# Low halves of w_in (from its seventh piece) and of the first layer's outputs: made by VectorE instead of GpSimd

## The chip, the cores and the metric

The kernel runs on one core of one Trainium2 chip. The metric is the device time of one execution in microseconds (us). The engines are TensorE (PE in the profile; PEld is its weight load), VectorE (DVE), ScalarE (ACT), GpSimd (POOL) and SyncE (SP), which here only issues DMAs. Each engine works through its own instructions strictly in the order of the program; only semaphores tie them together. "The time" below is the median of three runs; the profile is one further execution.

## What is computed

Three layers, chained:

```python
# attention with a decaying state, per batch and head (4 x 8, 768 steps, 48 wide)
f = sigmoid(f_logit)
state = f[t] * state + outer(k[t], v[t]);  y[t] = q[t] @ state
# x: the 3072 tokens, 384 wide
h = x @ w_in                      # 384 -> 2048
g = maximum(0.01 * h, h)
x2 = g @ w_out                    # 2048 -> 384
# then 8 experts, each with the 384 tokens that a greedy assignment gives it
out[mask] = maximum(x2[mask] @ w1[e], 0) @ w2[e]
```

The result has to be about as exact as float32. So the large products are made from pairs of 16-bit numbers: a value is split into a high half (the value rounded to float16) and a low half (what the rounding left out, again as float16), and a product is three matmuls, high by high, high by low and low by high. The low halves are the subject of this change.

## The kernel before

Tokens come in 24 tiles of 128. Three tiles make a group of 384, so there are eight groups. For each tile the attention runs as a chain over PE, ACT and DVE; its matmuls write to the tiles P (decays), A (scores), kT (turned keys), U (state update) and y, and DVE makes `ks`, `qs`, `de`, `St`, `am`, `ahl`, `vl` and `ys` for it. Its result is turned by a DMA into `xT`.

The first layer (`first`) goes over the 16 slices of 128 columns of w_in. Each slice f of a group is nine matmuls into one of three PSUM buffers `hp`; ACT scales it into `g`, DVE finishes the maximum there (which frees the buffer), and after every second f ACT makes the high half `gh` of both slices and POOL or DVE the low half `gl` of both. The second layer (`second`) takes, for each tile of tokens and each f, three matmuls into `xp` from `gh`, `gl` and the two halves of w_out, `wo`. Order on PE: layer one of group 0, layer one of group 1, layer two of group 0, layer one of group 2, and so on; attention of later tiles is put between.

The weights arrive as 64-bit words and are rebuilt to float32 by three integer instructions on DVE for each piece (`as_f32`: one TENSOR_SCALAR, two SCALAR_TENSOR_TENSOR, all 128 x 384; tiles `winu` and `woutu`). There are 16 pieces of w_in and 16 of w_out. For a piece of w_in (`split_win`) ACT then writes the high half `winh`, ACT writes the scaled float32 value once more into `wsc`, and POOL subtracts: `winl = wsc - winh`. For a piece of w_out (`split_wout`) ACT writes the high half and DVE the low half straight from the rebuilt words. The pieces pass through three load buffers (tag `ws`); a load into one waits until the piece three before has been rebuilt.

What sets the order: the opening (the string START) is written out by hand and kept in program order; it ends about where the first group's matmuls are under way. After it, a small driver hands out the work by due times, and a scheduler places each instruction by priorities and its own estimate of when operands are ready. So a changed instruction can move its neighbours.

Of the kernel before, what the change touches and what calls it, by code (L numbers as in the profile page):

```python
# [15 lines left out]
OP = mybir.AluOpType  # L16
# [5 lines left out]
SX, SWI, SG, SWO = 2.0 ** 10, 2.0 ** 7, 2.0 ** 10, 2.0 ** 8  # L22
# [69 lines left out]
def body(tc, qk, v, f_logit, w_in, w_out, w_gate, w1, w2, out):  # L92
    nc = tc.nc
    w_in, w_out = w_in.bitcast(I32), w_out.bitcast(I32)
    PE, DVE, ACT, POOL, SP = (InOrder(tc, e) for e in (nc.tensor, nc.vector, nc.scalar, nc.gpsimd, nc.sync))
# [10 lines left out]
    GW = 384  # L106
    RT = 3
    NWD = 0
    NWARM, WU = 0, 4
    MP = (1,)  # L110
    LEAD, PACE0, W0, POOLN, GLN, FT, KP, PB = 3, 1300.0, 1000.0, 8, 2, 8, 4, 3

    with ExitStack() as ctx:
        consts = ctx.enter_context(tc.tile_pool(name="consts", bufs=1))
# [15 lines left out]
        def mm(o, l, r, start, stop):  # L130
            return PE.matmul(o, l, r, start=start, stop=stop, skip_group_check=True)

        def copy(o, i, scale=1.0):
            return ACT.activation(o, i, AF.Copy, bias=0.0, scale=scale)
# [115 lines left out]
        winh = wpool.tile([128, KT, FF], F16)  # L250
        winl = wpool.tile([128, KT, FF], F16)
# [3 lines left out]
        def as_f32(t, name):  # L255

            sh = [128, t.shape[1], t.shape[2]]
            u = aw.tile(sh, I32, name=name + "u", tag="wu", bufs=WU)
            DVE.tensor_scalar(u, t[:, :, :, 1], 3, 0x3FFFFFFF, op0=OP.logical_shift_left, op1=OP.bitwise_and)
            DVE.scalar_tensor_tensor(u, t[:, :, :, 0], 29, u, op0=OP.logical_shift_right, op1=OP.bitwise_or)  # L260
            DVE.scalar_tensor_tensor(u, t[:, :, :, 1], -0x40000000, u, op0=OP.bitwise_and, op1=OP.bitwise_or)
            return u.bitcast(F32)

        def split_win(i):
            s = slice(i * WIC, (i + 1) * WIC)
            r = as_f32(w_in_s.pop(i), "win")
            yield
            t = aw.tile([128, KT, WIC], F32, name="wsc", tag="wsc", bufs=WU)
            copy(winh[:, :, s], r, SWI)
            copy(t, r, SWI)  # L270
            yield
            POOL.tensor_tensor(winl[:, :, s], t, winh[:, :, s], op=OP.subtract)
# [266 lines left out]
        def first(gi, nn, gx):  # L539
            xh, xl = gx[:, :KT], gx[:, KT:]  # L540
            N = 128 * nn
            gp = g2pool[0] if gi == LAST else gpool
            gh = gp.tile([128, NF, GW], F16, name="gh")
            gl = gp.tile([128, NF, GW], F16, name="gl")
            gh_[gi], gl_[gi] = gh, gl
            for f in range(NF):
                while ("in", f * NPC // NF) not in ready:
                    yield None
                fs = slice(128 * f, 128 * (f + 1))
                hp = psum.tile([128, GW], F32, name="hp", tag="mm", bufs=3)[:, :N]  # L550
                for c in range(KT):
                    mm(hp, winh[:, c, fs], xh[:, c, :N], c == 0, False)
                    yield N / 2.4
                    mm(hp, winh[:, c, fs], xl[:, c, :N], False, False)
                    yield N / 2.4
                    mm(hp, winl[:, c, fs], xh[:, c, :N], False, c == KT - 1)
                    if c < KT - 1:
                        yield N / 2.4
                a = SG / (SX * SWI)
                with tc.high_priority():  # L560
                    if f % 2 == 0:
                        g = work.tile([128, 2, GW], F32, name="g32")
                    t = g[:, f % 2, :N]
                    i = copy(t, hp, 0.01 * a)
                    fed.append((i, DVE.scalar_tensor_tensor(t, hp, a, t, op0=OP.mult, op1=OP.max)))
                    big[0] += 3 * KT
                    if f % 2:
                        s = slice(f - 1, f + 1)
                        copy(gh[:, s, :N], g[:, :, :N])
                        (POOL if gi == 0 or (gi < GLN and f % 4 == 1) else DVE).tensor_tensor(  # L570
                            gl[:, s, :N], g[:, :, :N], gh[:, s, :N], op=OP.subtract)
                yield N / 2.4

        def tok(n):
# [508 lines left out]

        live, complete = {}, set()
        names = dict(f=s0, v=s0v, p=s1, k=s2, a=s3, y=s4, x=s5, w=split_win)

        def group_x(n):
# [113 lines left out]
        def layer1():  # L1201
            for g in range(len(groups)):
                while not all(n in attended for n in groups[g]):
                    yield None
                started.append(g)
                if g == LAST:
                    while "experts" not in ready or "gate" not in ready:
                        yield None
                    ctxL.close()
                    g2pool.append(pool(ctxL, "g2", "left"))  # L1210
                    ctxP.close()
                    banks[0] = ctxP.enter_context(tc.tile_pool(name="banks2", bufs=1, space=bass.MemoryType.PSUM,
                                                               reuse_waits="tile"))
                beside = chain(*(logits(k) for k in LATE[:-1])) if g == LAST else iter(())
                for x in first(g, len(groups[g]), GX[g]):
                    yield x
                    if x is not None:
                        yield next(beside, 0.0)
                yield from beside
                done[0] = g + 1  # L1220
                if g > 0 and g - 1 not in LATE:
                    for m, n in enumerate(groups[g - 1]):
                        yield from second(g - 1, n, m)
            yield from logits(LAST)
# [105 lines left out]
```

## Time and profile before

| what | value |
| --- | --- |
| time, median of 3 runs | 785.66 us (784.7 to 787.34) |
| profiled execution, its own time | 781.42 us |
| its span, first to last instruction | 779.6 us |
| PE busy | 730.7 us (94%) |
| DVE busy | 558.8 us (72%) |
| ACT busy | 350.0 us (45%) |
| POOL busy | 142.7 us (18%), 158 instructions |

The profiled execution lies 4.2 us below the median of the runs, and 1.8 us of its time lie outside the span. The 72% of DVE is a mean over stages of very different kinds: from 47 to about 150 us DVE is busy nearly without a break, later it has room. POOL works in the opening and in this stage, and then not again before 400 us.

### The profile page before, as it was taken

What the parts mean: (1) busy time and instruction counts of PE and PEld (TensorE: products, weight loads), DVE (VectorE), ACT (ScalarE), POOL (GpSimd) and SP (SyncE); (2) the same over time, 40 slices, a digit from 0 to 9 for tenths busy, and PEclk for the clock granted to TensorE, in tenths of its full rate; (3) what the DMA queues carried; (4) which work ended last, traced back from release to release, by engine and by line L of the source; (5) the groups of instructions that cost most, each with busy time, mean ns of one, the idle gap of its engine ahead of it and who ended that gap; (6) DMA issues with size and microseconds to landing.
All of it is one profiled execution on the core that took longest, in us unless ns stands there. A gap on an engine that the chain in (4) does not pass through costs nothing.

```text
span 779.6 us, 15455 instructions
## 1 busy us (share of the span) xinstructions
PE 730.7 (94%) x5900; PEld 484.1 (62%) x5900; DVE 558.8 (72%) x1579; ACT 350.0 (45%) x732; POOL 142.7 (18%) x158
## 2 busy tenths in 40 slices
PE   6888998999999999998999999999989899999995
PEld 5756775677576577676666666555545455556663
DVE  5899999968966967966873958677685676873320
ACT  6566656557755754753663743000123123222320
POOL 5355312000000000000000001010243434535111
PEclk9899899999999999999999999999999999999998
DMA  9965544698897798998898500050475557665300
GB/s 258 249 162 164 161 133 125 152 276 219 237 249 213 210 309 191 250 249 221 238 272 230 166 2 2 23 192 22 148 224 155 177 158 168 228 198 174 107 31 30
DMA packets 111643, 135.90 MB, mean 174 GB/s; under 512 B 62929, under 2 KB 94674, under 8 KB 109522
## 3 DMA queue, kind: packets, MB, share of 16 engines
q1 hardware_dynamic: 106194, 100.31, 49.1%
q0 software_dynamic: 5376, 34.61, 13.1%
q8 instruction: 46, 0.75, 0.4%
q14 instruction: 27, 0.22, 0.1%
HBM read 86.52 MB, written 34.60 MB: 155 GB/s over the span
## 4 chain that ended last, share of the span: by engine, by line
PE 49%; DVE 25%; DMA 9%; issue 8%; ACT 5%; SPq 1%; POOL 1%; another core or an unknown queue 1%; POOLq 0%; ACTq 0%; DVEq 0%
PE hp L84 17%; PE xp L84 17%; PE yp L84 5%; DVE g L84 3%; PE y L84 3%; DVE winu L84 3%; DMA xw_s<-in_moe_w 3%; DMA fT<-in_f_logit 2%; DVE gl L84 2%; DVE woutu L84 2%; DMA turned<-x 2%; DVE xw_l L84 1%; PE P L84 1%; PE U L84 1%; PE c L84 1%
## 5 line engine op out<-in xcount | busy, mean ns | idle before, releaser
L84 PE MATMUL hp<-xT,winh 128*128 128x384 f16 x768 | 191.4, 329 | 11.8 <-DVE g L84 11.7
L84 PE MATMUL xp<-wo,gh 128*128 128x384 f16 x768 | 190.4, 326 | 0.8 <-DVE wo L84 0.8
L84 PE MATMUL hp<-xT,winl 128*128 128x384 f16 x384 | 126.3, 329 | 0.0
L84 PE MATMUL xp<-wo,gl 128*128 128x384 f16 x384 | 125.0, 326 | 0.0
L84 PEld LDWEIGHTS <-gh 128*128 128x128 f16 x912 | 83.9, 97 | 42.6
L84 PEld LDWEIGHTS <-winh 128*128 128x128 f16 x768 | 74.3, 99 | 57.3 <-issue 16.5
L84 PE MATMUL hp<-x2T,w1e 128*128 128x384 f16 x576 | 99.3, 325 | 0.7 <-ACT x2T L84 0.4
L84 PE MATMUL yp<-w2e,hh 128*128 128x384 f16 x384 | 94.4, 325 | 0.0
L84 ACT ACTIVATE g<-hp 128x384 f32<-128x384 f32 x152 | 73.0, 485 | 23.1 <-PE hp L84 21.5
L84 DVE SCALAR_TENSOR_TENSOR g<-hp,g 128x384 f32<-128x384 f32 x128 | 69.5, 552 | 8.2 <-ACT g L84 7.8
L84 PEld LDWEIGHTS <-w1e 128*128 128x128 f16 x576 | 52.3, 97 | 32.9 <-issue 1.1
L84 PEld LDWEIGHTS <-gl 128*128 128x128 f16 x528 | 48.7, 97 | 28.6 <-DVE gl L84 0.9
L84 ACT ACTIVATE gh<-g 128x768 f16<-128x768 f32 x64 | 53.9, 841 | 26.1 <-DVE g L84 25.4
L84 ACT ACTIVATE xw_h<-xw_s 128x768 f16<-128x768 f32 x64 | 53.2, 839 | 25.5 <-DMA xw_s<-in_moe_w 24.7
L84 POOL IOTA jp<- 128x128 f32 x2 | 0.5, 238 | 341.8 <-PE hp L84 341.7
L84 PE MATMUL yp<-w2e,hl 128*128 128x384 f16 x192 | 62.5, 325 | 0.0
L84 DVE TENSOR_TENSOR gl<-g,gh 128x768 f16<-128x768 f32 x52 | 49.7, 956 | 16.8 <-ACT gh L84 16.2
L84 DVE SCALAR_TENSOR_TENSOR xw_l<-xw_s,xw_h 128x768 f16<-128x768 f32 x64 | 60.2, 951 | 1.9 <-ACT xw_h L84 1.9
L84 ACT ACTIVATE hh<-hp 128x384 f16<-128x384 f32 x64 | 31.4, 491 | 62.2 <-PE hp L84 52.1
L84 ACT ACTIVATE x<-yp 128x384 f32<-128x384 f32 x24 | 11.8, 491 | 93.3 <-PE yp L84 75.1
L84 ACT ACTIVATE x<-xp 128x384 f16<-128x384 f32 x24 | 11.7, 489 | 92.0 <-PE xp L84 80.8
L84 PEld LDWEIGHTS <-winl 128*128 128x128 f16 x384 | 37.8, 98 | 22.9 <-issue 0.9
(265 smaller groups left out, 1228.3 us busy)
## 6 DMA issues: line engine op xcount, KB each, us to landing
xw_s<-in_moe_w SPq DMA_DIRECT2D x64, 384.0 KB, 4.0
qkT<-in_qk SPq DMA_DIRECT2D x48, 192.0 KB, 4.1
wout_s<-in_moe_w_out SPq DMA_DIRECT2D x16, 384.0 KB, 3.5
w1d<-xw_h SPq DMA_DIRECT2D x32, 192.0 KB, 4.2
w1d<-xw_l SPq DMA_DIRECT2D x32, 192.0 KB, 4.0
w2d<-xw_h SPq DMA_DIRECT2D x32, 192.0 KB, 4.3
w2d<-xw_l SPq DMA_DIRECT2D x32, 192.0 KB, 4.0
fT<-in_f_logit SPq DMA_DIRECT2D x24, 192.0 KB, 3.5
```

The lines of the kernel that those rows point to most:

```text
L84: i = f(*args, **kwargs)
```

## The change

GpSimd makes no low half of `gl` any more: in the first two groups it made 12 of 16 (all eight pairs of group 0, four of group 1), now DVE makes all. For w_in, pieces 0 to 5 stay as they are; from piece 6 on (10 pieces) DVE makes the low half in one instruction from the rebuilt words, as for w_out, and the second ACT copy (`wsc`) and the POOL subtraction go.

```diff
-    NWARM, WU = 0, 4
+    NWARM, WU, PLOW = 0, 4, 6
-    LEAD, PACE0, W0, POOLN, GLN, FT, KP, PB = 3, 1300.0, 1000.0, 8, 2, 8, 4, 3
+    LEAD, PACE0, W0, POOLN, FT, KP, PB = 3, 1300.0, 1000.0, 8, 8, 4, 3
 ...
             r = as_f32(w_in_s.pop(i), "win")
             yield
+            copy(winh[:, :, s], r, SWI)
+            if i >= PLOW:
+                DVE.scalar_tensor_tensor(winl[:, :, s], r, SWI, winh[:, :, s], op0=OP.mult, op1=OP.subtract)
+                return
             t = aw.tile([128, KT, WIC], F32, name="wsc", tag="wsc", bufs=WU)
-            copy(winh[:, :, s], r, SWI)
             copy(t, r, SWI)
             yield
             POOL.tensor_tensor(winl[:, :, s], t, winh[:, :, s], op=OP.subtract)
 ...
                         copy(gh[:, s, :N], g[:, :, :N])
-                        (POOL if gi == 0 or (gi < GLN and f % 4 == 1) else DVE).tensor_tensor(
-                            gl[:, s, :N], g[:, :, :N], gh[:, s, :N], op=OP.subtract)
+                        DVE.tensor_tensor(gl[:, s, :N], g[:, :, :N], gh[:, s, :N], op=OP.subtract)
```

The opening is the same up to the first slices of group 0. From there the order changes on PE, ACT, DVE and SP, and PE's order is the same again from the 133rd matmul into `xp` on (third tile of group 0), to the end of the kernel. Three places:

On DVE, at the first slices of group 0. `g32` is the tile `g`; `hp_…` are the PSUM buffers of the slices. Before:

```order
L84 SCALAR_TENSOR_TENSOR ahl_551<-A_521,mask_133 128x512
L84 SCALAR_TENSOR_TENSOR g32_578<-hp_565,g32_578 128x384
L84 SCALAR_TENSOR_TENSOR ahl_557<-A_522,mask_133 128x512
L84 SCALAR_TENSOR_TENSOR g32_578<-hp_581,g32_578 128x384
L84 SCALAR_TENSOR_TENSOR winu_607<-win_e_256,winu_607 128x384
L84 TENSOR_SCALAR winu_651<-win_s_292 128x384
L84 TENSOR_SCALAR winu_688<-win_s_294 128x384
L84 SCALAR_TENSOR_TENSOR winu_651<-win_s_292,winu_651 128x384
L84 SCALAR_TENSOR_TENSOR g32_620<-hp_595,g32_620 128x384
```

The same place on DVE now:

```order
L84 SCALAR_TENSOR_TENSOR ahl_551<-A_521,mask_133 128x512
L84 SCALAR_TENSOR_TENSOR g32_576<-hp_564,g32_576 128x384
L84 SCALAR_TENSOR_TENSOR winl_147<-winu_545,winh_146 128x3x128
L84 SCALAR_TENSOR_TENSOR ahl_556<-A_522,mask_133 128x512
L84 SCALAR_TENSOR_TENSOR g32_576<-hp_579,g32_576 128x384
L84 SCALAR_TENSOR_TENSOR winu_605<-win_e_256,winu_605 128x384
L84 SCALAR_TENSOR_TENSOR g32_616<-hp_593,g32_616 128x384
L84 TENSOR_SCALAR winu_647<-win_s_292 128x384
L84 TENSOR_TENSOR gl_563<-g32_576,gh_562 128x768
L84 SCALAR_TENSOR_TENSOR winl_147<-winu_605,winh_146 128x3x128
```

The low halves stand among the others, and the rebuilding of later pieces has moved behind the slices' `g`.

On PE, where layer two of group 0 comes to f = 15, the last piece of w_out. `xp_1459` was the first tile of tokens, `xp_1740` the second. Before, the last slice of the first tile, and then the second tile from its start:

```order
L84 LDWEIGHTS gh_563
L84 MATMUL xp_1459<-wo_148,gh_563 128x384
L84 LDWEIGHTS gl_564
L84 MATMUL xp_1459<-wo_148,gl_564 128x384
L84 LDWEIGHTS gh_563
L84 MATMUL xp_1740<-wo_148,gh_563 128x384
```

Now `xp_1439` is the first tile, `xp_1720` the second and `xp_1869` the third:

```order
L84 LDWEIGHTS gl_563
L84 MATMUL xp_1439<-wo_148,gl_563 128x384
L84 LDWEIGHTS gh_562
L84 MATMUL xp_1720<-wo_148,gh_562 128x384
L84 LDWEIGHTS gh_562
L84 MATMUL xp_1720<-wo_148,gh_562 128x384
L84 LDWEIGHTS gl_563
L84 MATMUL xp_1720<-wo_148,gl_563 128x384
L84 LDWEIGHTS gh_562
L84 MATMUL xp_1869<-wo_148,gh_562 128x384
```

When PE first needs the last piece of w_out, 45 matmuls into `xp` stood ahead of it and now 100 do: the second tile runs beside the first, slice by slice, and of the third the beginning. Ahead of it stand also one tile's P, A, kT, U and y more. On DVE the last low half of w_out has 29 more instructions ahead of it: 10 `winl`, 12 `gl` and 7 of the attention (two `am`, two `ahl`, `vl`, `St`, `de`).

On SP, at the loads of pieces 11 to 15 of w_in (`win_s`). Before:

```order
L84 DMA ld_v_771<-in_v 128x384
L84 DMA win_s_573<-in_moe_w_in 128x3x256
L84 DMA fT0_102<-in_f_logit 128x384
L84 DMA win_s_615<-in_moe_w_in 128x3x256
L84 DMA win_s_659<-in_moe_w_in 128x3x256
L84 DMA fT1_103<-in_f_logit 128x384
L84 DMA win_s_696<-in_moe_w_in 128x3x256
L84 DMA fT2_104<-in_f_logit 128x384
L84 DMA win_s_733<-in_moe_w_in 128x3x256
```

Now on SP:

```order
L84 DMA ld_v_761<-in_v 128x384
L84 DMA fT0_102<-in_f_logit 128x384
L84 DMA fT1_103<-in_f_logit 128x384
L84 DMA win_s_571<-in_moe_w_in 128x3x256
L84 DMA fT2_104<-in_f_logit 128x384
L84 DMA win_s_611<-in_moe_w_in 128x3x256
L84 DMA win_s_653<-in_moe_w_in 128x3x256
L84 DMA ld_v_900<-in_v 128x384
L84 DMA_TRANSPOSE xT_536<-ys_753 128x6x128
L84 DMA win_s_688<-in_moe_w_in 128x3x256
L84 DMA qkT0_85<-in_qk 48x1024 x2
L84 DMA win_s_723<-in_moe_w_in 128x3x256
```

The loads of `f_logit` (which wait until ACT has read the older contents) and a turn of `ys` stand ahead of pieces that they stood behind.

## Rows read from the trace of the kernel before

**Rows 1.** The page: busy time, share of the span and instructions of each engine.

```profile
PE 730.7 (94%) x5900; PEld 484.1 (62%) x5900; DVE 558.8 (72%) x1579; ACT 350.0 (45%) x732; POOL 142.7 (18%) x158
```

**Rows 2.** Busy time by stretch: PE, PEld, DVE, ACT, POOL; granted clock, DMA share, GB/s.

```profile
47.00:119.00 72.00, 63.84 (x434) 47.68 (x433) 71.10 (x123) 45.97 (x105) 28.99 (x21) 0.93 0.56 153
119.00:151.00 32.00, 28.28 (x248) 20.15 (x247) 31.84 (x63) 20.34 (x48) 3.96 (x2) 0.95 0.48 126
151.00:170.00 19.00, 19.00 (x164) 13.51 (x163) 14.33 (x27) 11.14 (x23) 0.00 (x0) 1.00 1.08 243
```

**Rows 3.** Waits from 47 to 140 us: total us, times, longest us.

```profile
PE hp L84 <- DVE g L84: 9.1, 7, 3.0
```

**Rows 4.** DVE in order of time: start us, us, instruction, count.

```profile
54.68 3.17 DVE L84 SCALAR_TENSOR_TENSOR winu<-win_s,winu 128x384 int32<-128x384 int32 x2
57.77 0.55 DVE L84 SCALAR_TENSOR_TENSOR g<-hp,g 128x384 f32<-128x384 f32 x1
```

**Rows 5.** POOL in order of time, the same stretch.

```profile
54.61 1.64 POOL L84 TENSOR_TENSOR gl<-g,gh 128x768 f16<-128x768 f32 x1 [0.65 <-ACT gh L84]
56.20 1.23 POOL L84 TENSOR_TENSOR winl<-wsc,winh 128x384 f16<-128x384 f32 x1
```

**Rows 6.** DVE by line, 47 to 140 us: count, busy us, mean ns, idle before.

```profile
L84 DVE SCALAR_TENSOR_TENSOR g<-hp,g 128x384 f32<-128x384 f32 x32 | 17.5, 551 | 0.4 <-ACT g L84 0.2
L84 DVE SCALAR_TENSOR_TENSOR woutu<-wout_s,woutu 128x384 int32<-128x384 int32 x26 | 16.9, 664 | 0.1
L84 DVE SCALAR_TENSOR_TENSOR winu<-win_s,winu 128x384 int32<-128x384 int32 x16 | 16.6, 1044 | 0.2
L84 DVE TENSOR_SCALAR woutu<-wout_s 128x384 int32<-128x384 int32 x14 | 7.2, 526 | 0.0
L84 DVE SCALAR_TENSOR_TENSOR wo<-woutu,wo 128x384 f16<-128x384 f32 x12 | 6.6, 551 | 0.0
L84 DVE SCALAR_TENSOR_TENSOR qs<-qkT,eq 128x512 f32<-128x512 f32 x5 | 5.6, 1120 | 0.0
L84 DVE TENSOR_TENSOR ks<-qkT,ek 128x512 f32<-128x512 f32 x5 | 4.3, 863 | 0.0
...
L84 DVE TENSOR_TENSOR de<-dn,ek 128x4 f32<-128x4 f32 x5 | 3.7, 733 | 0.0
```

**Rows 7.** The same, 140 to 240 us, where POOL does nothing.

```profile
L84 DVE TENSOR_TENSOR gl<-g,gh 128x768 f16<-128x768 f32 x8 | 7.7, 957 | 2.1 <-ACT gh L84 2.0
L84 DVE TENSOR_TENSOR ks<-qkT,ek 128x512 f32<-128x512 f32 x7 | 4.8, 688 | 4.0 <-PE kT L84 4.0
...
L84 DVE SCALAR_TENSOR_TENSOR qs<-qkT,eq 128x512 f32<-128x512 f32 x6 | 4.1, 691 | 6.0 <-PE y L84 5.9
...
L84 DVE SCALAR_TENSOR_TENSOR woutu<-wout_s,woutu 128x384 int32<-128x384 int32 x7 | 3.6, 554 | 0.0
...
L84 DVE TENSOR_TENSOR de<-dn,ek 128x4 f32<-128x4 f32 x7 | 1.1, 162 | 5.2 <-ACT ek L84 5.1
L84 DVE TENSOR_SCALAR woutu<-wout_s 128x384 int32<-128x384 int32 x2 | 0.7, 356 | 0.0
```

**Rows 8.** PE in order of time, layer two of group 0.

```profile
155.56 0.49 PE L84 MATMUL xp<-wo,gh 128*128 128x384 f16 x2
...
156.05 0.49 PE L84 MATMUL xp<-wo,gh 128*128 128x384 f16 x2
156.38 1.03 PE L84 MATMUL y<-St,qs 128*128 128x96 f32 x8
...
158.64 0.32 PE L84 MATMUL xp<-wo,gl 128*128 128x384 f16 x1
...
161.07 1.05 PE L84 MATMUL P<-span,ld 128*128 128x128 f32 x8
...
163.15 0.34 PE L84 MATMUL xp<-wo,gl 128*128 128x384 f16 x1
```

**Rows 9.** DMA issues: count, KB each, median us from issue to landing.

```profile
win_s<-in_moe_w_in SPq DMA_DIRECT2D x8, 384.0 KB, 3.7
```

## The prediction

> **What bounds the kernel now.** I read the busy times first. PE is busy 94% of the span [rows 1], so as a rule a saving counts only where PE waits. Cut into stretches [rows 2], one of them is different: from 47 to 119 us DVE is busy 71.10 of 72 us, from 119 to 151 us 31.84 of 32, while PE is idle 8.2 and 3.7 us. From 151 us on it is the other way: PE 19.00 of 19 us, DVE 14.33. So up to about 151 us VectorE sets the pace, behind that TensorE. The waits say the same: PE's longest are for `g`, which frees the PSUM buffer of the first layer, 9.1 us in seven waits [rows 3]. POOL works 28.99 + 3.96 = 33.0 us in this stage [rows 2], nearly all of it on the 22 instructions that the change takes away.
>
> At first sight the change puts work on the engine that is full. Why that is not all of it is to be seen in two stretches of the timeline, DVE's and POOL's. Two rebuilding instructions of `winu` take 3.17 us together [rows 4]; behind 140 us, where POOL is silent, one of the same shape takes 554 ns [rows 7]. While they run, POOL makes a `gl` (54.61 to 56.25 us) and a `winl` (56.20 to 57.43 us) [rows 5], and the pair ends 0.4 us after the second of these. DVE is busy in the profile, but it stands still until POOL is done.
>
> **What the change removes from DVE.** I sum this over 47 to 140 us, mean there [rows 6] less mean with POOL silent [rows 7]: `winu` 16 x (1044 - 554) ns = 7.8 us; `woutu` 26 x (664 - 554) = 2.9 and 14 x (526 - 356) = 2.4; `qs` 5 x (1120 - 691) = 2.1; `ks` 5 x (863 - 688) = 0.9; `de` 5 x (733 - 162) = 2.9. Together **19.0 us**. `g`, which reads PSUM, is not stretched (551 ns) [rows 6]. The loss cannot exceed POOL's own 33.0 us, and is not below zero; 19.0 is measured, so I take it.
>
> The Trainium skill has a rule for it (SBUF — State Buffer, section "Who interferes with whom"): VectorE and GpSimd share a pair of ports, a VectorE instruction with two SBUF inputs or in a 2-port mode contends with a GpSimd instruction that reads SBUF, and the later one blocks fully. The trace agrees on who is stretched and who not; taken at its worst, each POOL instruction blocking for its whole length, the rule would give 33.0 in place of 19.0 us and a time 14 us lower, which I do not use.
>
> **What it adds to DVE.** Durations on DVE overlap by 0.08 us: the pair of `winu` ends at 57.85 us and the next instruction starts at 57.77 [rows 4]. Twelve `gl` at 957 ns [rows 7], so 0.88 us of DVE's time each, are 10.5 us. Ten `winl`: the row nearest in kind is `wo`, made by the same operation from the same operands, 551 ns [rows 6], so 0.47 each and 4.7 us. Bounds: at 356 ns, the shortest 128 x 384 row here, it would be 2.8 us, at the unstretched 691 ns of a 128 x 512 row 6.1 us. Together **15.2 us** (13.3 to 16.6). ScalarE loses ten copies; it is busy 45.97 of 72 us [rows 2] and waits for others, so I count that at nothing. The opening keeps its six `winl` on POOL.
>
> By that alone DVE's stage is 19.0 - 15.2 = 3.8 us shorter.
>
> **What the new order moves.** The stage ends for PE when the last piece of w_out is there. On DVE seven more attention instructions now stand ahead of that: four of 128 x 512 at 0.61 us (as `qs` less the overlap), two of 128 x 384 at 0.47, one `de` of 0.08: 3.5 us. So DVE reaches this point at -19.0 + 15.2 + 3.5 = -0.3 us, the same time as before. But PE has more behind it by then. 100 matmuls into `xp` stand ahead of the last piece instead of 45. Three of them take 156.05 - 155.56 = 0.49 us [rows 8], so 55 are 9.0 us. One tile's U and y take 158.64 - 156.38 = 2.3 us, its P and A 163.15 - 161.07 = 2.1 us [rows 8]. Before, this work of **13.4 us** was done behind 151 us, where PE is the bound and every us of it counts; now it fills PE's waits inside the stage. Since PE's order is the same again from the 133rd matmul into `xp` to the end, what is gained there stays. There is room: PE was idle 11.9 us in the stage, and its granted clock of 0.93 and 0.95 of the full 2.4 GHz [rows 2] means up to 72 x 0.07 + 32 x 0.05 = 6.6 us lost in stretches at 1.2 GHz, behind its gaps. The best case is then -0.3 - 13.4 = -13.7 us.
>
> **What takes some of it back.** DVE and PE now have about equally much to do in the stage, and DVE no longer has stalls in which others get ahead. New waits of DVE: each `gl` needs ScalarE's `gh` first. Behind 140 us such waits are 2.1 us in 8 [rows 7], so 12 cost 3.2 us. `winl` needs `winh` in the same way, but `wo` shows no wait of that kind (0.0) [rows 6]. For the balance with PE I add one wait of the longest size that this pair of engines now has, 3.0 us [rows 3]. Together 6.2 us; bounds are 0 and, if all is given back, 13.7. The moved loads on SP I count at nothing: a load of a piece of w_in lands 3.7 us after its issue [rows 9] and, by DVE's order, is wanted some 17 instructions, 8 us, after its buffer is free.
>
> **The sum.** -13.7 + 6.2 = -7.5 us. The profiled execution of 781.42 us would become 773.9; it lies 4.2 us below the median, and I take the difference to stay: 785.66 - 7.5 = **778.2 us**. Its own range: 1 us of new waits gives 773.0, 10 us give 782.0.
>
> **Rivals.**
> (a) The order brings nothing, because PE's extra matmuls wait for the same pieces as before; only DVE's net counts: -3.8 us, 781.9 us. For it: the second tile's matmuls need each piece too. Against: they come when the first tile has waited for the piece already.
> (b) The new waits give everything back: 785.7 us. For it: each slice now passes DVE, ScalarE, DVE and PE in turn, in order, and buffers for only three slices stand between. It decides from 11 us of new waits on.
> (c) Slower: SP's order. SP issues in order; two loads of `f_logit`, which wait for ScalarE, and a turn, which waits for DVE, now stand ahead of pieces 11 to 15. If each of the five comes one landing of 3.7 us [rows 9] late, DVE stands still 18.5 us: -7.5 + 18.5 = +11.0, 796.7 us. The kernel becomes slower from the third late piece on. Against it: the 8 us of room above.
> (d) The stretching is not POOL's, so the change doesn't do what it should: 19.0 us stay, 797.2 us. Against it [rows 4 to 7]: the same instructions are short wherever POOL is silent. The Trainium skill (Perfetto Trace Analysis, section "Optimizing Scalar/DVE Operations") says that with VectorE saturated some of its work may be worth moving to ScalarE or GpSimd, which would make this change the wrong way round; it adds that between VectorE and GpSimd it might not help, because of their port, and the trace bears out the second half.
>
> **Chances.** The forecast 0.52, (a) 0.18, (b) 0.15, (c) 0.12, (d) 0.03. Leaving out (c) and (d), and a little of (b), the range is 772.5 to 786.0 us. About 0.3% (2.4 us) is what a measurement of this kernel can tell from no change: faster is the forecast and (a), 0.70; the same (b), 0.15; slower (c) and (d), 0.15.
>
> **What would show it.** In the profile of the changed kernel `winu` and `woutu` should be near 554 and 356 ns, `de` near 160, and no POOL work stand between 47 and 400 us; ten `winl` on DVE near 551 ns. PE's idle time from 47 to 151 us should fall from 11.9 to about 5 us, and the clock be granted more fully. The 133rd matmul into `xp`, behind which PE's order is the same again, stands where the last stretch of [rows 2] ends, at about 170 us; it should come 7 to 8 us earlier, and the distance from there to the end stay the same. If DVE shows waits for ScalarE or PE of 10 us and more in the stage, it is (b); if it waits for loads of `win_s`, (c). If the point of the 133rd matmul is early but the end is not, then a later stage was bound by something else than PE, and the whole chain of this sum is wrong behind 170 us.

## The result, and the profile after

The changed kernel takes **776.41 us** (median of six runs, 771.42 to 780.64), the kernel before 785.19 us in the six runs beside it (784.09 to 787.34). The ratio is 0.9894 with an interval of 0.9849 to 0.9938: faster, by 8.8 us by the medians. The forecast was 778.2 us, 7.5 us less than before. In the comparisons further down, three single runs (one of the kernel before, two of winl_only) were slow, at a low granted clock, and their medians leave them out.

The profiled execution of the changed kernel took 780.38 us, its span is 778.6 us. Its busy times, to be held against [rows 1]:

```profile
PE 740.0 (95%) x5900; PEld 488.5 (63%) x5900; DVE 553.8 (71%) x1601; ACT 346.4 (44%) x722; POOL 110.1 (14%) x136
```

DVE has 22 instructions more and is busy 5.0 us less. The stretches of [rows 2], in the same columns:

```profile
47.00:119.00 72.00, 70.82 (x499) 51.09 (x499) 65.31 (x134) 47.34 (x108) 1.20 (x1) 0.93 0.50 138
119.00:151.00 32.00, 29.91 (x251) 20.48 (x249) 30.81 (x66) 19.56 (x45) 0.00 (x0) 1.00 0.60 166
151.00:170.00 19.00, 18.05 (x152) 12.56 (x151) 18.38 (x40) 10.87 (x23) 0.00 (x0) 1.00 0.71 186
```

From 47 to 151 us PE is now idle 1.2 + 2.1 = 3.3 us (11.9 before), and DVE, which had no room, is idle 7.9 us. Part of this belongs to the late opening of this profile (below); in a later profile of the changed kernel (after_fourth, below) PE is idle 4.1 and DVE 4.2 us in the same window, so neither is clearly the bound any more. The groups of DVE from 47 to 140 us, against [rows 6] and [rows 7]:

```profile
L84 DVE SCALAR_TENSOR_TENSOR g<-hp,g 128x384 f32<-128x384 f32 x32 | 17.6, 552 | 4.6 <-ACT g L84 4.6
L84 DVE TENSOR_TENSOR gl<-g,gh 128x768 f16<-128x768 f32 x16 | 15.2, 950 | 0.0
L84 DVE SCALAR_TENSOR_TENSOR woutu<-wout_s,woutu 128x384 int32<-128x384 int32 x20 | 10.6, 551 | 0.0
L84 DVE SCALAR_TENSOR_TENSOR winu<-win_s,winu 128x384 int32<-128x384 int32 x16 | 8.7, 549 | 0.0
L84 DVE SCALAR_TENSOR_TENSOR winl<-winu,winh 128x384 f16<-128x384 f32 x10 | 5.5, 550 | 1.1 <-ACT winh L84 1.1
...
L84 DVE SCALAR_TENSOR_TENSOR ys<-y,ys 128x384 f16<-128x384 f32 x6 | 3.3, 553 | 3.3 <-ACT ys L84 3.3
L84 DVE TENSOR_SCALAR woutu<-wout_s 128x384 int32<-128x384 int32 x10 | 3.3, 354 | 0.0
...
L84 DVE SCALAR_TENSOR_TENSOR qs<-qkT,eq 128x512 f32<-128x512 f32 x4 | 2.7, 686 | 0.0
L84 DVE TENSOR_TENSOR ks<-qkT,ek 128x512 f32<-128x512 f32 x4 | 2.7, 686 | 0.0
...
L84 DVE TENSOR_TENSOR de<-dn,ek 128x4 f32<-128x4 f32 x4 | 0.6, 160 | 0.0
```

Every instruction that was stretched has the length that it had before only where POOL was silent: `winu` 549 ns (1044), `woutu` 551 and 354 (664 and 526), `qs` 686 (1120), `ks` 686 (863), `de` 160 (733). The moved low halves cost what the sum said, 950 and 550 ns. `gl` waits for nothing; DVE's waits are for other things.

**What the first profile hides.** The 133rd matmul into `xp` should have come 7 to 8 us earlier, and it comes at 168.53 in place of 170.25 us, 1.7 us. The reason lies ahead of the change, in the opening. Stretches of the opening, columns as in [rows 2], first of the kernel before, then of the changed one:

```profile
29.50:33.00 3.50, 3.50 (x24) 3.18 (x25) 3.40 (x7) 2.16 (x5) 0.91 (x1) 0.50 1.78 306
33.50:53.00 19.50, 18.89 (x150) 14.58 (x149) 16.72 (x31) 13.63 (x33) 6.50 (x5) 1.00 0.62 147
```

```profile
29.50:33.00 3.50, 3.41 (x20) 2.89 (x20) 3.40 (x7) 2.99 (x7) 0.91 (x1) 0.50 1.09 344
33.50:53.00 19.50, 19.50 (x100) 17.07 (x100) 11.87 (x23) 8.18 (x21) 2.38 (x2) 0.50 0.55 113
```

In both the granted clock is 0.50 (1.2 GHz) at 30 us. Before, it is back at 2.4 GHz by 33.5 us; in the changed kernel PE works on at 1.2 GHz up to 53 us, without a gap, through instructions that are the same in both. So layer one of group 0 starts 7.2 us later, at 50.73 in place of 43.51 us.

To take this out I count from a mark behind it: the 19th matmul into `hp`, which opens the third slice. Three rows of PE and one of DVE then tell the stage: that matmul, the first into `xp`, the last low half of w_out on DVE, and the 133rd into `xp`. In the kernel before:

```profile
46.44 0.49 PE L84 MATMUL hp<-xT,winh 128*128 128x384 f16 x2
...
132.69 0.49 PE L84 MATMUL xp<-wo,gh 128*128 128x384 f16 x2
...
150.10 0.55 DVE L84 SCALAR_TENSOR_TENSOR wo<-woutu,wo 128x384 f16<-128x384 f32 x1
...
170.25 0.49 PE L84 MATMUL xp<-wo,gh 128*128 128x384 f16 x2
```

In the changed kernel, in a later profile (after_fourth, below) whose opening ran at 2.4 GHz throughout:

```profile
45.30 0.49 PE L84 MATMUL hp<-xT,winh 128*128 128x384 f16 x2
...
117.11 0.48 PE L84 MATMUL xp<-wo,gh 128*128 128x384 f16 x2 [0.32 <-DVE g L84]
...
151.85 0.56 DVE L84 SCALAR_TENSOR_TENSOR wo<-woutu,wo 128x384 f16<-128x384 f32 x1 [0.18 <-ACT wo L84]
...
159.08 0.49 PE L84 MATMUL xp<-wo,gh 128*128 128x384 f16 x2
```

The same differences for all kernels of this study, from their traces, in us from the 19th matmul into `hp`. The second column is the end of the last low half of w_out on DVE, the third counts the matmuls into `xp` that had started by then, and "to before" is the change of the fourth:

| kernel | first `xp` | last piece of w_out | `xp` matmuls started by then | 133rd `xp` | to before |
| --- | --- | --- | --- | --- | --- |
| before | 86.2 | 104.2 | 45 | 123.8 | |
| changed, first profile | 71.9 | 107.2 | 101 | 113.7 | -10.1 |
| changed, three later profiles | 71.6 to 71.8 | 106.8 to 107.1 | 101 | 113.4 to 113.8 | -10.0 to -10.4 |
| pool_memset | 68.8 | 87.6 | 46 | 107.1 | -16.7 |
| pool_back | 87.4 | 124.9 | 101 | 131.2 | +7.4 |
| xp_in_order | 71.3 | 109.9 | 46 | 126.2 | +2.4 |
| order_alone | 86.9 | 103.6 | 62 | 120.8 | -3.1 |
| gl_only, two profiles | 70.9, 72.5 | 102.0, 103.7 | 90 | 111.0, 112.6 | -12.8, -11.2 |
| winl_only | 82.1 | 107.9 | 75 | 120.8 | -3.0 |
| no_pool | 72.6 | 108.0 | 104 | 112.9 | -10.9 |

So the change is worth 10 us in its stage, in four profiles of it, while the execution first profiled had lost 8.4 us ahead of the mark (54.89 in place of 46.44 us). Behind the 133rd matmul the distance to the end of the span is nearly the same, 609.35 us before and 610.07 after. So the first profile itself is 1.0 us shorter than the one of before, and the reading of 10 us rests on the mark.

### The profile page after: what moved, and what is told of

It reads as the page before. It is cut to its first block, busy times and chain, and to the rows that moved or that the text cites. A ratio compares the mean times of both kernels' runs of the same rounds, so it can differ in the third digit from the quotient of the medians.

```text
span 778.6 us, 15455 instructions
## 1 busy us (share of the span) xinstructions
PE 740.0 (95%) x5900; PEld 488.5 (63%) x5900; DVE 553.8 (71%) x1601; ACT 346.4 (44%) x722; POOL 110.1 (14%) x136
## 4 chain that ended last, share of the span: by engine, by line
PE 61%; DVE 18%; DMA 8%; issue 7%; ACT 2%; POOL 1%; another core or an unknown queue 0%; SPq 0%; POOLq 0%; ACTq 0%; DVEq 0%
PE hp L84 25%; PE xp L84 17%; PE yp L84 6%; PE y L84 4%; DMA fT<-in_f_logit 3%; PE A L84 2%; DVE woutu L84 2%; PE P L84 2%; DMA turned<-x 2%; DVE g L84 2%; PE U L84 1%; PE c L84 1%; DVE gl L84 1%; DMA qkT<-in_qk 1%; DMA turned<-wo 1%
## 5 line engine op out<-in xcount | busy, mean ns | idle before, releaser
L84 PE MATMUL hp<-x2T,w1e 128*128 128x384 f16 x576 | 100.9, 329 | 0.8 <-ACT x2T L84 0.7
L84 DVE TENSOR_TENSOR gl<-g,gh 128x768 f16<-128x768 f32 x64 | 61.1, 954 | 15.4 <-ACT gh L84 14.6
```

The source lines that it names most:

```text
L84: i = f(*args, **kwargs)
```

## The experiments

Each kernel was measured beside runs of the kernel before on the same chip; every time is a median.

**The change again.** after_again, after_third and after_fourth are the changed kernel itself.

> The changed kernel once more, for what differs between its own executions. Theory 1 (the stage from 47 to 151 us is shorter by the overlap of PE with VectorE's work): in every execution the distance from the first matmul into hp to the 133rd into xp is some 10 us shorter than before, and a spread of 771 to 781 us comes from elsewhere. Theory 2 (the clock in the opening): the times fall into two heaps some 7 us apart, with a mean granted clock near 0.987 and near 0.975; a profile of the upper heap shows 20 us and more at 1.2 GHz between 29 and 53 us, one of the lower heap some 7 us of it. If the spread has nothing to do with the clock, the clock is the same in both heaps.

> The kernel of the change once more, beside the three others on one chip. By the two runs before it lies 8.8 to 14.9 us under the kernel before; between 762 and 778 us. The open point is the opening: in both profiles of it so far TensorE's granted clock is 1.2 GHz for some 24 us from 29 to 53 us, in work that is the same in both kernels, where the kernel before shows 7 us. If that is chance, this profile may show it shorter, and the first matmul into hp then comes near 44 us in place of 51; if it belongs to the kernel, it stands here again.

> The kernel of the change beside those two. 7 to 15 us less than the kernel before on this chip; the stage 113.5 us in the profile.

Measured: 767.49 us against 782.21 of before (0.9806, interval 0.9779 to 0.9833), 767.46 against 776.86 (0.9894, 0.9860 to 0.9927), 770.01 against 782.25 (0.9869, 0.9825 to 0.9914): 14.7, 9.4 and 12.2 us less. The stage took the same in every profile (the table). The times of single runs go with their mean granted clock, as theory 2 of after_again has it: in the first comparison the three runs of 771.4 to 773.7 us have 0.986 to 0.988, the three of 779.1 to 780.6 us 0.974 to 0.977. The 1.2 GHz stretch of the opening stood in the second and third profile again, and not in the fourth:

```profile
33.50:53.00 19.50, 18.42 (x139) 13.44 (x139) 17.67 (x36) 13.98 (x34) 2.09 (x2) 1.00 0.88 176
```

So the long stretch does not belong to the code. xp_in_order and pool_back have the opening of the changed kernel, and in their profiles it is as short as in that of before: the 19th matmul stands at 46.63 and 46.73 us. What sets its length was not tried.

**Is the stretching GpSimd's, and what does it cost?** pool_memset is the kernel before, its order too, with GpSimd writing zeros in place of the 22 subtractions, so these low halves are left out of the products (shown for `gl`; the ten `winl` likewise):

```diff
-                        (POOL if gi == 0 or (gi < GLN and f % 4 == 1) else DVE).tensor_tensor(
-                            gl[:, s, :N], g[:, :, :N], gh[:, s, :N], op=OP.subtract)
+                        if gi == 0 or (gi < GLN and f % 4 == 1):
+                            POOL.memset(gl[:, s, :N], 0.0)
+                        else:
+                            DVE.tensor_tensor(gl[:, s, :N], g[:, :, :N], gh[:, s, :N], op=OP.subtract)
...
```

> The kernel before, with its order, but the 22 subtractions on GpSimd (12 gl, 10 winl from piece 6 on) are replaced by memsets to zero of the same tiles, so these low halves are left out of the result. GpSimd then writes but reads nothing from SBUF. Theory 1 (GpSimd's reads stretch VectorE by 19.0 us): winu and woutu fall to near 554 and 356 ns, VectorE reaches the last piece of w_out some 19 us earlier, PE becomes the bound and the time falls by 9 to 13 us, as much as PE's idle time there allows. Rival (the stretching has another cause): the durations stay at 1044 and 664 ns and the time within 2 us of before.

Measured: 763.52 against 782.21 us (0.9749, 0.9715 to 0.9783), 18.7 us less, of which 16.7 are in the stage. That is more than the 9 to 13 us that were expected of this run. DVE from the mark to the end of the last low half of w_out, first in the kernel before, then here, in the columns of [rows 2]:

```profile
46.44:150.65 104.21, 92.33 (x681) 67.97 (x679) 103.13 (x186) 66.52 (x152) 33.51 (x23) 0.93 0.54 146
49.58:137.18 87.60, 84.92 (x682) 63.15 (x680) 84.70 (x186) 66.58 (x156) 4.04 (x5) 1.00 0.64 174
```

The same 186 instructions keep DVE busy 103.1 - 84.7 = 18.4 us less, against 19.0 us in the sum; its waits grow by 1.8 us. DVE's groups from 47 to 140 us:

```profile
L84 DVE SCALAR_TENSOR_TENSOR woutu<-wout_s,woutu 128x384 int32<-128x384 int32 x32 | 17.1, 553 | 0.1
...
L84 DVE SCALAR_TENSOR_TENSOR winu<-win_s,winu 128x384 int32<-128x384 int32 x16 | 8.7, 550 | 0.2
```

pool_back is the changed kernel with GpSimd making the same 22 subtractions beside DVE's, into a scratch tile that nobody reads:

```diff
+                POOL.tensor_tensor(t, r, winh[:, :, s], op=OP.subtract)
...
+                            POOL.tensor_tensor(u[:, :, :N], g[:, :, :N], gh[:, s, :N], op=OP.subtract)
```

> The changed kernel in its own order, and beside it GpSimd does its 22 subtractions again, into a scratch tile that nobody reads. Theory 1: winu, woutu, de, qs and ks are stretched again by about 19 us in all, on top of the 15.2 us of VectorE's new work; VectorE is the bound of the whole stage and the time is 12 to 18 us above the changed kernel. Rival (the gain comes from the order alone, stretching does not matter): within 3 us of the changed kernel.

Measured: 789.2 against 782.21 us (1.0084, 1.0054 to 1.0114), 21.7 us above the changed kernel beside it, more than the 12 to 18 expected; the stage is 17.7 us longer. Who is held up depends on what stands beside GpSimd's work: here it is the new instructions too, `gl` 1557 ns in place of 950, and not `qs`, `ks` and `de` (678, 682 and 153 ns), which the expectation had named. `g`, which reads PSUM, again is not:

```profile
L84 DVE TENSOR_TENSOR gl<-g,gh 128x768 f16<-128x768 f32 x16 | 24.9, 1557 | 0.0
L84 DVE SCALAR_TENSOR_TENSOR g<-hp,g 128x384 f32<-128x384 f32 x32 | 17.5, 549 | 2.5 <-ACT g L84 2.3
L84 DVE SCALAR_TENSOR_TENSOR winu<-win_s,winu 128x384 int32<-128x384 int32 x16 | 11.1, 699 | 0.0
L84 DVE SCALAR_TENSOR_TENSOR winl<-winu,winh 128x384 f16<-128x384 f32 x10 | 8.8, 883 | 0.0
```

The scratch work also holds the buffers that it reads for longer, but that is not the loss. From the mark to the last low half of w_out, in the fourth profile of the changed kernel and here:

```profile
45.30:152.41 107.11, 102.22 (x802) 73.10 (x801) 101.90 (x214) 69.00 (x158) 0.91 (x1) 1.00 0.56 159
46.73:171.60 124.87, 107.62 (x803) 75.73 (x801) 120.77 (x214) 69.50 (x158) 37.80 (x23) 0.96 0.48 137
```

The same 214 instructions keep DVE busy 18.9 us longer, and its idle time is 4.1 us in place of 5.2. Work whose results nobody uses costs the whole gain and more.

Is it GpSimd's reading of SBUF, or would writing do it too? The mean of 550 ns in pool_memset does not tell: a memset waits for no operand, and 18 of the 22 had run by 35 us, ahead of the stage. Only four ran beside DVE's work there:

```profile
52.88 3.14 POOL L84 MEMSET gl<- 128x768 f16 x4 [2.40 <-DMA fT<-in_f_logit]
```

```profile
52.74 1.24 DVE L84 TENSOR_SCALAR winu<-win_s 128x384 int32<-128x384 int32 x2
...
54.84 1.01 DVE L84 SCALAR_TENSOR_TENSOR winu<-win_s,winu 128x384 int32<-128x384 int32 x2
```

Beside them the instructions with two SBUF inputs keep their length (1.01 us for two of 0.54 that overlap), and two TENSOR_SCALAR, with one input, take 1.24 us in place of 0.63 (two of 354 ns, less the overlap). So the reading holds up the two-input instructions; for the one-input form writing does too, as far as one such place shows.

**Does the new order count, or VectorE's relief alone?** xp_in_order is the changed kernel with layer two of group 0 held in the program's order, as it was before; DVE's order is the changed kernel's:

```diff
+        def kept(gi, i):
+            if gi == 0:
+                tc.keep_in_program_order(i)
+            return i
...
-                mm(xp, gh[:, f, s], wo[:, f, 0], f == 0, False)
+                kept(gi, mm(xp, gh[:, f, s], wo[:, f, 0], f == 0, False))
```

> The changed kernel, but the matmuls of group 0's second layer are kept in the order of the program, so that the second tile of tokens does not start before the first has ended: 45 matmuls into xp stand ahead of the last piece of w_out instead of 100. VectorE's work is the same. Theory 1 (the second tile fills PE's waits): 9.0 us of PE's work go back behind the stage, the time is 6 to 9 us above the changed kernel, near that of before. Rival (a) (the order brings nothing): within 2 us of the changed kernel.

Measured: 784.12 against 782.21 us (1.0024, 0.9991 to 1.0058), 16.6 us above the changed kernel beside it: the whole gain is gone, and more than the 6 to 9 us expected. The first matmul into `xp` comes as early as in the changed kernel (71.3 us from the mark). Then PE has only the first tile and the attention, and waits with both. Between there and the 133rd:

```profile
117.00:151.00 34.00, 26.06 (x207) 20.31 (x206) 30.70 (x65) 17.16 (x40) 0.00 (x0) 0.85 0.54 157
151.00:173.00 22.00, 19.66 (x140) 12.10 (x140) 15.88 (x32) 9.49 (x20) 0.00 (x0) 0.92 0.83 180
```

PE's longest waits from 117 to 170 us are:

```profile
PE y L84 <- DVE ahl L84: 3.6, 3, 1.2
PE A L84 <- DVE qs L84: 2.7, 2, 1.4
PE xp L84 <- ACT wo L84: 2.6, 3, 1.6
```

So more of it waits for attention results than for pieces of w_out; with the second tile in its order PE had work in these places. PE is idle 7.94 + 2.34 = 10.3 us (3.1 in the fourth profile of the changed kernel), and in these stretches, with the idle time, the granted clock is 0.85 and 0.92 in the mean: parts of them ran at 1.2 GHz, by estimate worth another 34 x 0.15 + 22 x 0.08 = 6.9 us, which the expectation had left out. In that profile of the changed kernel the same part has 1.00.

order_alone is the reverse: the kernel before, GpSimd's work as it was, and the first two tiles of group 0 written side by side, slice by slice:

```diff
             for f in range(NF):
...
+                for (n, m), xp in zip(nm, xps):
+                    s = slice(128 * m, 128 * (m + 1))
+                    mm(xp, gh[:, f, s], wo[:, f, 0], f == 0, False)
...
+                    if g == 1:
+                        yield from second_of(0, nm[:2])
```

> The kernel before, GpSimd's work as it was, but TensorE's matmuls into xp for the first two tiles of group 0 written side by side, slice by slice: 90 of them stand ahead of the last piece of w_out in place of 45. VectorE has as many instructions ahead of that piece as before (247 in place of 250). Theory of the sum: VectorE reaches the last piece at about the same time in the changed kernel too (-0.3 us), and the gain is TensorE's work moved beside it; then the order alone gives the same: 45 x 0.163 = 7.3 us less than before, 6 to 9. Rival: while GpSimd holds VectorE up, TensorE gets its hp slices so late that the moved matmuls find no gaps, and the relief of VectorE is needed as well: 0 to 3 us less. From the 19th matmul into hp to the 133rd into xp it took 123.8 us before and 113.4 to 113.6 in the three profiles of the changed kernel.

Measured: 786.97 against 782.25 us (1.0052, 1.0021 to 1.0082), slower by 4.7 us. From the 133rd matmul to the end it takes 619.1 us where the changed kernel on that chip takes 608.4. The edit also changed the order of later work, and what of that costs the time is not shown; so its time is no measure of the order alone, and I go by the stage. That is 3.1 us shorter, but 8 P, 16 A, 4 kT and 6 `pg` matmuls that stood ahead of the 133rd now stand behind it. By [rows 8] P and A are 2.1 us, so at most 1 us is left: the rival (0 to 3 us) holds, not the theory of 6 to 9. The reason is in the table: without relief PE comes to `xp` at 86.9 us, and DVE finishes the last piece at 103.6. In these 17 us PE is busy with 62 matmuls into `xp` and the attention, and there is no gap to fill. From 132 to 151 us, in the kernel before and then in order_alone:

```profile
132.00:151.00 19.00, 17.94 (x184) 13.94 (x182) 18.85 (x39) 10.69 (x28) 1.91 (x1) 0.99 0.43 108
```

```profile
132.00:151.00 19.00, 18.69 (x163) 13.61 (x162) 18.91 (x39) 9.53 (x21) 1.79 (x1) 0.97 0.33 94
```

The relief makes the gap (PE comes 14.4 us earlier, DVE's last piece 2.9 us later), and the order fills it. Each alone brings next to nothing, as long as VectorE makes the low halves itself; in pool_memset, where nobody makes them, its last piece comes 16.6 us earlier, and with the old order too the kernel gains.

**Which low halves?** gl_only moves only `gl` (the `winl` stay on GpSimd), winl_only only `winl`:

```diff
-                        (POOL if gi == 0 or (gi < GLN and f % 4 == 1) else DVE).tensor_tensor(
+                        DVE.tensor_tensor(
```

```diff
+            if i >= PLOW:
+                DVE.scalar_tensor_tensor(winl[:, :, s], r, SWI, winh[:, :, s], op0=OP.mult, op1=OP.subtract)
+                return
```

> The kernel before with one part of the change alone: all gl are made by VectorE; the ten winl stay on GpSimd, with their second ScalarE copy. Theory (GpSimd's reads hold VectorE up): in the timeline of before the 12 gl on GpSimd (1.64 us each) lie beside most of the stretched instructions, the 10 winl (1.23 us each) beside fewer; by that about 15 of the 19 us of stretch are gl's. VectorE gets back 15 and does 10.5 more. 89 matmuls into xp stand ahead of the last piece of w_out here, 44 more than before, 44 x 0.163 = 7.2 us. So 9 to 12 us less than before, most of the gain. Rival (each low half costs VectorE what GpSimd worked on it, in equal shares): 12 x 1.64 = 19.7 of 33 us of GpSimd's time go, that is 60% of 19 = 11.4 us of stretch, net -0.9 us on VectorE, and with the order 5 to 8 us less. In the profile: winu mean still above 554 ns, de between 160 and 733 ns.

> All gl on VectorE, the ten winl on GpSimd as before, once more. In the first run its stage from the 19th matmul into hp to the 133rd into xp took 111.0 us, 2.5 less than the changed kernel. If winl on VectorE (4.7 us) costs more than what GpSimd's ten subtractions still stretch once gl is gone, this is the faster kernel again, by 1 to 4 us; if that was chance, it stands within 1 us of the changed kernel.

> The kernel of the change with gl split between GpSimd and VectorE as before: only the ten winl have moved, and the second ScalarE copy is gone. Theory: about 4 of the 19 us of stretch go and 4.7 us of winl come, so VectorE's stage is as long as before; 74 matmuls into xp stand ahead of the last piece, 29 more than before, 29 x 0.163 = 4.7 us. So 2 to 5 us less than before. Rival (equal shares): 10 x 1.23 = 12.3 of 33 us go, 7 us of stretch, net -2.4 us; with the order 5 to 7 us less. Rival (ScalarE's ten copies matter, which the prediction counted at nothing): 5 us of ScalarE's stage go and the time falls by more than 7 us. The two parts alone should add up to about the whole change, unless the order that comes with both together is what counts.

Measured: gl_only 765.85 against 776.86 us (0.9859, 0.9823 to 0.9895) and 769.47 against 782.25 (0.9832, 0.9797 to 0.9867), so 11.0 and 12.8 us less; winl_only 775.29 against 776.86 (0.9979, 0.9948 to 1.0010), 1.6 us less, no difference that can be measured. So ScalarE's ten copies, which winl_only takes away as well, are not worth the 7 us of that rival. The groups of gl_only that are still stretched, from 47 to 140 us:

```profile
L84 DVE SCALAR_TENSOR_TENSOR winu<-win_s,winu 128x384 int32<-128x384 int32 x16 | 10.0, 642 | 0.0
...
L84 DVE TENSOR_SCALAR winu<-win_s 128x384 int32<-128x384 int32 x8 | 3.4, 444 | 0.0
...
L84 DVE TENSOR_TENSOR de<-dn,ek 128x4 f32<-128x4 f32 x4 | 1.3, 337 | 0.0
```

With `gl` gone GpSimd's ten remaining subtractions stretch these by 16 x 0.09 + 8 x 0.09 + 4 x 0.18 = 2.9 us, and the other groups not at all. Moving them as well costs DVE 4.7 us. So by this the second half of the change costs about 1.8 us in the stage: the last piece is ready at 102.0 and 103.7 us in gl_only, at 107 in the whole change, and the 133rd matmul comes 1.2 to 2.6 us earlier. In the total time the two are not told apart (1.6 and 0.5 us, less than either interval); gl_only_again had called a difference within 1 us chance. The expectation by the timeline held for gl_only (9 to 12 less; 11.0 and 12.8), and winl_only came out just under its 2 to 5. The two parts do not add up: in the stage they bring 11.2 to 12.8 and 3.0 us, the whole change 10. Why is not shown.

**GpSimd out altogether.** no_pool takes the change to the opening as well:

```diff
-    NWARM, WU, PLOW = 0, 4, 6
-    MP = (1,)
-    LEAD, PACE0, W0, POOLN, FT, KP, PB = 3, 1300.0, 1000.0, 8, 8, 4, 3
+    NWARM, WU, PLOW = 0, 4, 0
+    MP = ()
+    LEAD, PACE0, W0, POOLN, FT, KP, PB = 3, 1300.0, 1000.0, 8, 8, 0, 3
```

> The change taken to its end: also the six winl of the opening and the other GpSimd arithmetic ahead of the experts are made by VectorE. Theory: in the opening from 20 to 47 us VectorE is busy only part of the time (31.56 of 47 us in the changed kernel) and waits for loads, so what GpSimd's reads cost it there is mostly hidden: 0 to 4 us less than the changed kernel beside it. Rival: the opening too is bound by VectorE's stalls, and 5 us or more go. Rival: work of the opening on GpSimd is really parallel there, as the waits are for loads, and moving it adds 6 x 0.47 = 2.8 us: up to 3 us more than the changed kernel.

Measured: 768.68 against 776.86 us (0.9901, 0.9867 to 0.9936), beside 767.46 for the changed kernel. The 1.2 us more are within the intervals, so nothing is gained, and whether the work of the opening costs anything on VectorE cannot be told.

## Why the prediction was right, and where its sizes were off

**The bound.** Right. The stage was VectorE's; made shorter on VectorE, it shortened the kernel (pool_memset: 18.7 us, 16.7 of them in the stage).

**The 19.0 us.** Right, term by term in the groups above; in pool_memset 18.4 us of VectorE's busy time came back. Rival (d) falls with pool_memset and pool_back. The Trainium skill's rule (SBUF — State Buffer, "Who interferes with whom") also says that a VectorE instruction with two SBUF inputs contends with a GpSimd instruction that reads SBUF, not with one that only writes it. The four memsets in the stage of pool_memset agree (two `winu` beside them in 1.01 us). At its worst, blocking for the whole 33.0 us, it would have been too much.

**The 15.2 us added.** Right: 950 ns each for `gl` and 550 for `winl`, less the overlap.

**DVE at the last piece of w_out.** Here a term is off. The sum had -0.3 us from the work and 6.2 us of new waits, so 5.9 us later than before; measured it is 2.9 (104.2 to 107.1 us from the mark). By the windows shown above, DVE's idle time up to there went from 1.1 to 5.2 us in the fourth profile, so the new waits are 4.1 us (4.7 to 5.2 in the other three), and its busy time fell from 103.1 to 101.9 us, 1.2 us in place of 0.3. The makeup of the waits was wrong too: 3.2 us of them were to be `gl` waiting for `gh`, and `gl` waited 0.0. DVE's waits in the fourth profile, 47 to 140 us:

```profile
DVE g L84 <- ACT g L84: 2.9, 4, 1.1
DVE winl L84 <- ACT winh L84: 1.1, 1, 1.1
DVE ys L84 <- ACT ys L84: 0.5, 1, 0.5
```

Together 4.5 us, no single one over 1.1. (In the other three profiles this window shows 8.3 to 9.0 us, but 3.0 of that is one wait for `ys` ahead of the mark.) I had carried the waits of `gl` over from a stage where PE is the bound and DVE stands ready for each operand; here DVE is busy with other work, and `gh` is there before its turn.

**The moved work.** Nearly right: 13.4 us were to move inside the stage. The 133rd matmul comes 10.1 us earlier from the mark although the last piece comes 2.9 us later, so 13.0 us moved; 101 matmuls into `xp` stand ahead of that piece. What I did not see is why there is room. I counted PE's idle time and its lost clock all over the stage (11.9 + 6.6 us). Nearly all of that idle time lies ahead of the first `xp`, most of it in the waits for `g`, and order_alone shows that matmuls into `xp` cannot fill it. The room is made by the relief: layer one of the first two groups ends 14.4 us earlier.

**The sum.** -13.0 + 2.9 = -10.1 us in the stage against -7.5 forecast; the term that was mis-sized is the new waits, 6.2 against 4.1. The total came out at 8.8, 14.7, 9.4 and 12.2 us less in four comparisons, 11.3 in the mean. That the first lies so near to 7.5 is in part luck: half of its runs stood at the lower mean clock. The clock of the opening is one reason why the four differ; how much of each difference is the clock's cannot be settled from the mean clock of the runs that were not profiled.

**The rivals.** (a) falls as a forecast, but what it feared is real: with the old order on PE the gain is zero (xp_in_order), so without the new one the relief would have been lost in waits. (b) did not come: PE's 9.1 us of waiting for `g` [rows 3] are 0.5 in the fourth profile, 47 to 151 us.

```profile
PE hp L84 <- DVE g L84: 0.5, 2, 0.4
```

(c) did not come either. In the first profile of the changed kernel a `win_s` lands later than in [rows 9] (3.8 to 7.0 us in the four profiles, against 3.7), but no instruction of DVE waits for one from 47 to 140 us:

```profile
win_s<-in_moe_w_in SPq DMA_DIRECT2D x8, 384.0 KB, 5.4
```

## What to carry to other kernels

When VectorE is busy without a break beside GpSimd, compare the same instruction where GpSimd works and where it is silent, before work is moved from one to the other: here 22 GpSimd instructions cost VectorE more (19.0 us) than doing their work itself (15.2 us). Where the relieved engine takes over as much work as it is rid of, so that its last result comes no earlier, the relief is worth something only if the engine behind it has other work in its order to start with; ask what stands there next, and what that needs. And count from a mark behind the opening, since one profile can lose there as much as the change gains.

## What was not expected of the hardware

The granted clock of the opening: the same instructions ran at 1.2 GHz up to about 53 us in three profiles of the changed kernel (in the first with PE busy 19.50 of 19.50 us) and at 2.4 GHz in the fourth, a difference of 9.6 us at the mark (54.89 and 45.30 us). And the distance from the 133rd matmul to the end of the span was 610.1, 606.2, 602.6 and 608.4 us in these four profiles of one kernel, while kernels measured side by side lay closer (602.6 to 603.9 in one set of four, 606.2 to 609.5 in another; order_alone with its 619.1 stands apart); so only kernels that were measured side by side should be compared. Neither has an explanation here.
